# Attention with rotary embedding and a gated feed-forward layer: the scores of the first two blocks issued product by product, head against head, ahead of the other queries' transposes

## The chip, the cores and the metric

The kernel runs on one core of one Trainium2 chip. The metric is the device time of one execution in microseconds (us). The three executions of the kernel before took 718.72, 719.28 and 720.00 us; the median is 719.28 us. The profile is of one further execution of 719.76 us.

## The reference, cut to what matters

There are 4 batches, 8 heads, 576 positions and a head width of 64. Queries and keys are rotated, the scores are a softmax over 576 keys, and the result, laid out as 2304 tokens of 512 numbers, goes through a gated layer of width 1536:

```python
q_rot, k_rot = rotate(q), rotate(k)
scores = (1 / sqrt(64)) * q_rot @ k_rot.T
attn = exp(scores - max(scores)); attn = attn / (sum(attn) + 1e-9)
x = (attn @ v)            # as 2304 x 512
out = (silu(x @ w_gate) * (x @ w_val)) @ w_out
```

## The kernel before, in words

The 32 (batch, head) combinations are worked in 16 pairs of heads. A pair has 9 blocks of 128 queries: blocks 0 to 7 are four groups of queries for each of the two heads in turn (block 0 is head 0, block 1 is head 1, both of the first 128 queries), and block 8 holds the last 64 queries of both heads. Head 0 of a pair stands on partitions 0 to 63 and head 1 on partitions 64 to 127 of the tile `N`, which holds a rounded high part (index 1) and the rest, the low part (index 0), of the rotated and transposed queries and keys.

For each block TensorE makes the scores (`scores`): three terms, high by high, high by low and low by high, each as two products of 288 keys, added up in one PSUM buffer of two banks. There are two such buffers (`sc_p`, two in turn). VectorE takes the row maximum from the buffer (`peak`), ScalarE reads it again for the exponential with a row sum (`exp`), and then the buffer is free. Four TensorE transposes (`trans`) turn the result for the product with the values (`pv`).

The first blocks, among them 0 to 5, are "direct": each product contracts the 64 partitions of its head alone, so its stationary operand is 64x128. Later blocks stack the terms on 128 partitions (`QK`, `QZ`, `BD`), which `qk_stack` fills by eight DMAs on SyncE's queue (L313 to L320).

`start` (L210) writes the work of the first pair up to block 2 by hand, for all engines. The relevant part of it: `warm` (L223) issues idle 128x128 products on the identity to keep TensorE at work; `hi` and `lo` (L302, ScalarE; L306, VectorE) copy a transposed piece from PSUM into `N` as high part and low part; the first 128 queries and all keys are ready first, and the other queries are transposed at L253 after the rotation of them is done on GpSimd. The lists `warm` and `direct` of `PLAN` (L27) give the counts. Both score buffers serve VectorE's rotation as scratch (`tp`, `td`) before block 0 takes one of them.

After `start` a loop over all 144 blocks issues the steps. The order on GpSimd is the written one throughout, on SyncE up to block 47 and on TensorE up to block 8; the order of the others' instructions (VectorE's and ScalarE's from the loop on, TensorE's from block 9) is set at build time by a planner, which runs the program on a timeline of its own and takes what is ready by priority. From the end of the attention on, the order is written out again.

## Time and profile before

| | |
|---|---|
| median of three executions | 719.28 us |
| the profiled execution, its own time | 719.76 us |
| span of the profile, first to last instruction | 717.9 us |
| TensorE busy | 697.0 us (97%) |
| VectorE busy | 540.6 us (75%) |
| ScalarE busy | 409.6 us (57%) |
| GpSimd busy | 476.8 us (66%) |
| mean granted TensorE clock | 0.994 |

Busy times are of the engine's own work; PE is TensorE's products, PEld its loads of the stationary operand, DVE VectorE, ACT ScalarE, POOL GpSimd, SPq the DMA issues of SyncE. A product's busy time overlaps its neighbours', so the pitch from one to the next is read from the chain of waits, which counts each stretch once.

### The profile page before, as it was taken

Reading aid. Unit: us, or ns where it says so; the run is one execution under the profiler, and the core shown is the slowest. Engines: PE = TensorE matmul, PEld = TensorE weight load, DVE = VectorE, ACT = ScalarE, POOL = GpSimd, SP = SyncE. Lnnn points to the kernel's source line nnn. Section 1 sums busy time; section 2 is a strip of 40 time slices with the busy share of each in tenths; the row PEclk is TensorE's granted clock in tenths of the full one; section 3 lists DMA queues with packets and bytes.
Section 4 is the critical chain, followed back from the end, with each engine's and each line's share of the span. In section 5 each row is a group of like instructions: output and inputs, shape, how many; then the busy total and the mean of one; then the engine's idle time right before and its main releaser. Section 6 shows DMA issues by size and latency. Waiting matters only on the chain.

```text
span 717.9 us, 12738 instructions
## 1 busy us (share of the span) xinstructions
PE 697.0 (97%) x4342; PEld 656.7 (91%) x4342; DVE 540.6 (75%) x884; ACT 409.6 (57%) x892; POOL 476.8 (66%) x473
## 2 busy tenths in 40 slices
PE   7999999999999999998899999999999999999997
PEld 6999999999999998988899999999999877888887
DVE  5889898898898887848988778778677893464451
ACT  5889988888888886357433534424243332432331
POOL 8899799999999966649966576655675767200000
PEclk9999999999999999999999999999999999999999
DMA  6798899779887896862355555645638865787671
GB/s 195 195 232 204 218 227 253 199 202 249 233 215 196 201 269 165 248 202 101 121 168 171 177 163 173 193 147 165 185 115 272 280 245 169 306 284 223 205 220 30
DMA packets 111330, 143.86 MB, mean 200 GB/s; under 512 B 17809, under 2 KB 86049, under 8 KB 111265
## 3 DMA queue, kind: packets, MB, share of 16 engines
q1 hardware_dynamic: 106576, 137.64, 67.5%
q10 hardware_dynamic: 4688, 5.39, 2.3%
q8 instruction: 35, 0.57, 0.3%
q14 instruction: 31, 0.25, 0.1%
HBM read 76.35 MB, written 42.54 MB: 166 GB/s over the span
## 4 chain that ended last, share of the span: by engine, by line
PE 64%; DMA 10%; POOL 10%; DVE 8%; ACT 5%; issue 2%; SPq 1%; ACTq 0%; DVEq 0%; POOLq 0%
PE ch L824 28%; PE ch L941 13%; PE sc L343 7%; PE pv L459 6%; PE tr L419 5%; DMA HF<-hf 3%; PE ch L892 2%; POOL t L200 1%; DMA raw<-in_moe_w_gate_dram 1%; DMA QK<-N 1%; POOL rot L202 1%; DMA ht<-sv 1%; POOL rot L201 1%; PE tr L283 1%; POOL Xab L628 1%
## 5 line engine op out<-in xcount | busy, mean ns | idle before, releaser
L358 DVE TENSOR_REDUCE nmt<-sc 128x1 f32<-128x576 f32 x144 | 108.1, 751 | 20.0 <-PE sc L343 18.4
L376 ACT ACTIVATE E<-sc,nmt 128x576 f32<-128x576 f32 x128 | 97.3, 760 | 1.6 <-DVE nmt L358 1.4
L808 POOL TENSOR_TENSOR u<-u,z 128x384 f32<-128x384 f32 x30 | 30.5, 1018 | 72.9 <-DVE sg L808 72.9
L419 PE MATMUL tr<-ident,E 128*128 128x128 f32 x512 | 77.1, 273 | 0.5 <-DVE ET1l L421 0.2
L419 PEld LDWEIGHTS tr<-ident,E 128*128 128x128 f32 x512 | 61.1, 141 | 3.4 <-PE tr L283 1.3
L827 ACT COPY c<-ch 128x384 f32<-128x384 f32 x30 | 14.4, 480 | 84.7 <-PE ch L824 50.2
L200 POOL TENSOR_TENSOR t<-X,tab 128x256 f32<-128x256 f32 (+2 forms) x94 | 54.2, 597 | 10.1 <-DMA X<-in_qk_dram 6.4
L343 PE MATMUL sc<-QK 128*128 128x288 f32 x240 | 58.6, 325 | 1.7 <-ACT E L376 0.4
L420 ACT CAST ET2h<-tr 128x512 fp32r<-128x512 f32 x80 | 47.1, 589 | 15.5 <-PE tr L419 15.4
L421 DVE TENSOR_TENSOR ET2l<-tr,ET2h 128x512 fp32r<-128x512 f32 x80 | 53.1, 682 | 2.2 <-ACT ET2h L420 2.0
L678 DVE TENSOR_TENSOR hl<-hg,hh 128x384 fp32r<-128x384 f32 x44 | 25.8, 587 | 37.6 <-ACT hh L678 37.6
L941 PE MATMUL ch<-Oh,hh 128*128 128x512 f32 (+1 forms) x144 | 54.0, 375 | 0.0
L941 PE MATMUL ch<-Oh,hl 128*128 128x512 f32 (+1 forms) x144 | 53.9, 374 | 0.0
L941 PE MATMUL ch<-Ol,hh 128*128 128x512 f32 (+1 forms) x144 | 53.8, 374 | 0.0
L343 PE MATMUL sc<-N,QZ 128*128 128x288 f32 x240 | 51.3, 295 | 0.0
L202 POOL TENSOR_TENSOR rot<-rot,t 128x512 f32<-128x512 f32 (+2 forms) x47 | 47.0, 1000 | 3.7
L421 DVE TENSOR_TENSOR ET1l<-tr,ET1h 128x512 fp32r<-128x512 f32 x64 | 43.0, 685 | 6.8 <-ACT ET1h L420 6.5
L201 POOL TENSOR_TENSOR rot<-X,tab 128x512 f32<-128x512 f32 (+2 forms) x47 | 47.0, 1001 | 0.0
L808 DVE TENSOR_TENSOR sg<-ch,u 128x384 f32<-128x384 f32 x60 | 33.4, 556 | 16.5 <-PE ch L824 13.3
L678 ACT CAST hh<-hg 128x384 fp32r<-128x384 f32 x44 | 22.6, 514 | 39.3 <-DVE hg L928 39.3
L420 ACT CAST ET1h<-tr 128x512 fp32r<-128x512 f32 x64 | 36.9, 597 | 13.0 <-PE tr L419 13.0
L459 PE MATMUL pv<-ET2h,VS 128*128 128x320 f32 x128 | 40.7, 328 | 1.0 <-ACT ET2h L420 0.9
(413 smaller groups left out, 2418.9 us busy)
## 6 DMA issues: line engine op xcount, KB each, us to landing
QK<-N SPq DMA_DIRECT2D x64, 288.0 KB, 4.4
hg<-ht SPq DMA_DIRECT2D x22, 768.0 KB, 6.8
HF<-hf SPq DMA_DIRECT2D x12, 896.0 KB, 5.1
X<-in_qk_dram SPq DMA_DIRECT2D x15, 576.0 KB, 4.9
yd<-Y SPq DMA_DIRECT2D x31, 256.0 KB, 4.4
ht<-sg SPq DMA_DIRECT2D x20, 384.0 KB, 3.7
hf<-sg SPq DMA_DIRECT2D x20, 384.0 KB, 3.8
ht<-sg SPq DMA_DIRECT2D x20, 320.0 KB, 3.1
```

Of the source, the lines that this page charges most:

```text
L200: e.tensor_tensor(out=sel(t2, u), in0=sel(x, w), in1=tb(Sn, u), op=ALU.mult)
L201: e.tensor_tensor(out=o, in0=x, in1=tb(C, slice(0, D)), op=ALU.mult)
L343: nc.tensor.matmul(ps[:, g, 0:288], l, rr[:, o + g * 288:o + (g + 1) * 288], start=(x == 0), stop=(x == len(terms) - 1))
L358: nc.vector.tensor_reduce(out=nmcol, in_=ps[:, :, 0:288], axis=AX.XY, op=ALU.max, negate=True)
L376: nc.scalar.activation(out=E.rearrange("p (a b) -> p a b", a=2), in_=ps[:, :, 0:288], func=ACTF.Exp, bias=nmcol, scale=1.0, accum_out=self ...
L419: nc.tensor.transpose(ps[:, c], E[:, o + c * 128:o + (c + 1) * 128], self.ident)
L420: nc.scalar.copy(dst[0], src)
L421: nc.vector.tensor_tensor(out=dst[1], in0=src, in1=r32(dst[0]), op=ALU.subtract)
L459: nc.tensor.matmul(st["ps"][:, 0:w], VS[:, sl, :], t, start=(x == 0), stop=(x == last))
L808: add = lambda e, out, in0, in1: e.tensor_tensor(out=out, in0=in0, in1=in1, op=ALU.add)
L824: nc.tensor.matmul(acc, l[:, w, c * 128:(c + 1) * 128], r, start=(n == 0), stop=(n == 5))
L941: self.nc.tensor.matmul(ps, l[:, f], r[:, z], start=(n == 0), stop=(n == 3 * NFF - 1))
```

## The change

The scores of blocks 0 and 1 are no longer two calls of `scores` with the three transposes of the other queries (L253) between them. One new function takes both score buffers at once and issues the twelve products in turn: for each term and each half of the keys first head 0's, into the first buffer, then head 1's, into the second. The transposes follow behind all twelve. `hi`, `lo`, both `peak`, both `exp`, the idle products and everything on other engines keep their places in the written order. The argument of the first old call that could issue idle products behind its first term had a count of zero (`w[4]`).

```diff
         warm(w[3])
-        self.scores(0, False, lambda x: warm(w[4]) if x == 0 else None)
+        self.scores2()
         self.peak(0)
         ps = tr()
         for i in range(1, 4):
             T(ps[:, i * 128:(i + 1) * 128], rf[:, i * 128:(i + 1) * 128], self.ident)
-        self.scores(1, False)
         hi(ps[:, 128:512], 192, 384)
         lo(ps[:, 128:512], 192, 384)
         self.peak(1)
...
+    def scores2(self):
+        N = self.N[0]
+        ps = []
+        for n in range(2):
+            ps.append(self.sc_p.tile([128, 1024], FP32, name="sc").rearrange("p (a b) -> p a b", a=2))
+            self.sc[n] = ps[n]
+        for t, (x, y) in enumerate(((1, 1), (1, 0), (0, 1))):
+            for g in range(2):
+                for h in range(2):
+                    hs, ko = slice(64 * h, 64 * h + 64), (640, 576)[h]
+                    self.nc.tensor.matmul(ps[h][:, g, 0:288], N[hs, x, 64:192],
+                                          N[hs, y, ko + g * 288:ko + (g + 1) * 288], start=(t == 0), stop=(t == 2))
```

## Rows read from the trace of the kernel before

**Rows 1.** The page: busy time by engine, and the last chain's shares by engine.
```profile
PE 697.0 (97%) x4342; PEld 656.7 (91%) x4342; DVE 540.6 (75%) x884; ACT 409.6 (57%) x892; POOL 476.8 (66%) x473
...
PE 64%; DMA 10%; POOL 10%; DVE 8%; ACT 5%; issue 2%; SPq 1%; ACTq 0%; DVEq 0%; POOLq 0%
```
**Rows 2.** The chain of waits, 9 to 25 us: start, duration, what.
```profile
9.46 0.98 PE sc L343 x6
10.44 0.48 PE tr L253 x3
10.91 0.98 PE sc L343 x6
11.90 0.42 PE pv L223 x2
12.32 0.98 PE sc L343 x6
13.30 0.59 PE tr L419 x4
...
15.47 0.44 PE tr L283 x4
...
23.55 0.80 PE sc L343 x6
24.35 0.44 PE tr L419 x4
```
**Rows 3.** The timeline, all engines, 9.3 to 14 us: start, duration, what [idle before].
```profile
9.38 0.82 PEld L343 LDWEIGHTS sc<-N 64*128 64x128 f32 x6
...
10.47 0.76 DVE L358 TENSOR_REDUCE nmt<-sc 128x1 f32<-128x576 f32 x1 [0.69 <-PE sc L343]
...
10.95 0.48 ACT L302 CAST N<-tr 128x384 fp32r<-128x384 f32 x1 [1.02 <-PE tr L253]
...
11.33 0.75 ACT L376 ACTIVATE E<-sc,nmt 128x576 f32<-128x576 f32 x1
11.46 0.73 SPq L313 DMA_DIRECT2D QK<-N  x1
11.46 0.56 DVE L306 TENSOR_TENSOR N<-tr,N 128x384 fp32r<-128x384 f32 x1 [0.23 <-ACT N L302]
...
11.94 0.76 DVE L358 TENSOR_REDUCE nmt<-sc 128x1 f32<-128x576 f32 x1
11.96 0.20 ACT L376 ACTIVATION_READ_ACCUMULATOR E<-sc,nmt 128x1 f32 x1
...
12.25 0.82 PEld L343 LDWEIGHTS sc<-N 64*128 64x128 f32 x6
...
12.73 0.74 ACT L376 ACTIVATE E<-sc,nmt 128x576 f32<-128x576 f32 x1 [0.57 <-DVE nmt L358]
```
**Rows 4.** The timeline of VectorE, 8 to 10 us: the scratch's last reader.
```profile
8.34 0.29 DVE L202 TENSOR_TENSOR rot<-rot,sc 128x128 f32<-128x128 f32 x1
```
**Rows 5.** The timeline of SyncE's queue, 0 to 50 us, and of GpSimd.
```profile
22.02 0.60 SPq L313 DMA_DIRECT2D QK<-N  x1
...
30.21 0.59 SPq L169 DMA_DIRECT2D X<-in_qk_dram  x1
...
35.22 0.60 POOL L200 TENSOR_TENSOR t<-X,tab 128x64 f32<-128x64 f32 x2 [1.97 <-DMA X<-in_qk_dram]
```
**Rows 6.** The whole chain: block 8's scores of the sixth to eighth pair.
```profile
109.68 0.80 PE sc L343 x6
...
126.13 0.80 PE sc L343 x6
...
142.60 0.80 PE sc L343 x6
```
**Rows 7.** Stretches: busy time (instructions) of each engine, PEclk, DMA share, GB/s.
```profile
66.00:82.50 16.50, 15.48 (x122) 14.82 (x121) 15.87 (x29) 15.32 (x40) 12.60 (x14) 1.00 0.88 211
...
148.50:165.00 16.50, 16.49 (x132) 16.23 (x132) 14.50 (x24) 14.57 (x38) 15.78 (x21) 1.00 0.84 222
```
**Rows 8.** A stretch with a long TensorE wait, and that wait (us, times, longest).
```profile
274.00:278.00 4.00, 2.59 (x23) 2.35 (x21) 4.00 (x7) 3.87 (x10) 3.31 (x4) 1.00 0.41 129
...
PE ch L776 <- ACT Et L376: 1.4, 1, 1.4
```

## The prediction

> **What bounds the kernel now.** I read the page first: TensorE (PE) is busy 97% of the span, and the chain that ended last runs 64% on it [rows 1]. The reader should take from this only that a microsecond taken from TensorE may count, not that it does here: the change touches 3 us out of 718, and what it is worth is read from those. So the second view is the chain of waits around the change. From 9.46 to 13.9 us it is TensorE alone: scores of block 0, three transposes, scores of block 1, two idle products, scores of block 2, first transposes of the exponentials [rows 2]. Third is the timeline of all engines in the same stretch, since a chain shows one releaser and hides those that came a moment earlier [rows 3]. There the load for block 2's scores starts at 12.25 us, while ScalarE finishes the exponential of block 0, whose buffer block 2 needs, at 11.96 + 0.20 = 12.16 us. TensorE and ScalarE are 0.09 us apart at this point: two limits that are nearly equal, and the change relieves one of them. The second chain behind it is: transposes at L253, ScalarE's high copy (10.95), the exponential of block 0 (11.33), the free buffer (12.16). The maximum of block 0 (10.47 to 11.23) comes into the exponential just ahead of the copy's end.

> **The change part by part.** All sums go by the pitch of products, from the chain.

> *What it removes.* A block of six products with 64 contracted rows takes 0.98 us, a block of six of the same 288 columns with 128 rows takes 0.80 us (the blocks at 9.46 and 23.55) [rows 2]: 0.133 us a product, and 0.18 us more for turning to 64 rows. Four transposes behind a 64-row block take 0.59 us, in a row of transposes 0.44 us (at 13.30 and 15.47) [rows 2]: 0.15 us for turning back, and 0.11 us for a transpose, each with a load of its own. One trip out and back, 0.33 us, goes away, because blocks 0 and 1 are now one 64-row stretch.

> *What it adds: the length of the stretch of twelve products.* No row shows two products of different halves of the partitions next to each other, so the length has to be bounded. Lowest: each pair runs side by side, 6 x 0.133 + 0.18 = 0.98 us, as long as one block before. Highest of the plain cases: one after the other, 12 x 0.133 + 0.18 = 1.78 us. Between them: the products overlap but each needs its own load, and loads come no closer than the transposes show, 12 x 0.11 + 0.18 = 1.50 us. A fourth is a turn at each change of half: 11 changes at 0.15 to 0.18 us on top of 1.78, which is 3.4 to 3.8 us. I take 1.50 us, because the nearest row in which every product brings a new load is the transposes' 0.11 us.

> [...]

> *What is late then.* The three transposes stood behind six products and now stand behind twelve. They start later by the stretch less 0.98 us: 0 (side by side), 0.52 (loads), 0.80 (one by one), 2.4 to 2.8 (turns). Before, nothing else held them. With them move ScalarE's high copy, hence VectorE's low copy and second maximum (L306, 11.46; L358, 11.94), the exponential of block 0, which stands behind the copy in ScalarE's queue, the exponential of block 1 (12.73), and the first DMA of the stack on SyncE (L313, 11.46) [rows 3]. The buffer of block 0 comes free at 12.16 + shift, and 0.03 us later block 2's scores can start: 12.19 + shift against 12.25, so the net shift is -0.06, +0.46, +0.74 or +2.3 to +2.7 us. The other way into the exponential is milder: head 0's last product stands one place before the end, so the maximum ends at 11.23 + 0.52 - 0.11 = 11.64 us, before the copy frees ScalarE at 11.33 + 0.52 = 11.85.

> So what the change gains on TensorE, the second block's scores out of the way early and a 0.33 us trip saved, becomes a wait before block 2: in my case the three transposes (0.48 us) and the idle products end about 0.6 us before the buffer is free. The gain cannot be had, since no stretch of twelve can be shorter than block 0's six, and the chain transposes, copy, exponential starts behind it. That is why even full overlap is worth 0.06 us.

> *What costs nothing.* The stretch needs both buffers at once; their scratch use ends at 8.34 + 0.29 = 8.63 us [rows 4], before 9.38. The low parts of the keys and queries are needed only from the fifth and ninth product, later in the queue than before. No DMA and no GpSimd instruction is moved past another. The added wait of TensorE is short against one that this trace holds without harm: in 274 to 278 us it was busy 2.59 of 4.00 us, with one wait of 1.4 us, and the granted clock stayed at 1.00 [rows 8].

> *Does the shift reach the end?* Behind 13 us everything hangs on TensorE, ScalarE and VectorE of this chain; SyncE's second stack (22.02) and with it the load of the fourth pair's queries (30.21), on which GpSimd waits 1.97 us at 35.22 [rows 5], move with it. Later TensorE is full: 16.49 of 16.50 us in 148.5 to 165 [rows 7], so nothing there swallows or gives back. I let the 0.46 us through whole.

> Sum: the profiled execution's own 719.76 + 0.46 = 720.2 us. That execution lies 0.48 us over the median of the runs shown, so against the median: 719.28 + 0.46 = **719.7 us**. About 0.2%, 1.44 us, is what a measurement of this kernel tells from no change, so this is no change.

> **The rivals.**

> [...] *One by one (the change does not do what its order suggests):* +0.74, 720.0 us. For it: the pitch of 0.133 us has so far held for 64 and 128 rows alike. [...]

> *A turn at each change of half, slower.* If TensorE empties itself between the halves as it does between 64 and 128 rows, the twelve products take 3.4 to 3.8 us, block 2 starts 2.3 to 2.7 us late, and the time is 721.6 to 722.0 us. For it: the turns of 0.15 and 0.18 us exist. Against: they are seen only where the number of rows changes. It decides from about 0.06 us a change on: 0.74 + 11 x 0.064 = 1.44 us.

> *The plan falls another way.* VectorE's and ScalarE's order from the loop on and TensorE's from block 9 are made by a planner, whose view of the start is changed too. From 109.68 on, block 8's scores come every 16.45 us (126.13, 142.60) [rows 6]; from 23.55 to 109.68 [rows 2, 6] five pairs took 86.13 us, 3.9 us more than five such periods. In that part TensorE has holes (15.48 of 16.50 us in 66 to 82.5, where VectorE is busy 15.87 [rows 7]). That is 0.8 us a pair. A luckier order there could return the loss of two to five pairs, 1.6 to 3.9 us off the 719.7: 715.8 to 718.1 us. An unluckier one could lose as much again for two to four pairs, 1.6 to 3.1 us: 721.3 to 722.8 us. For both: ties of a tenth of a microsecond decide such orders. Against both: TensorE returned to the same period after every disturbance before.

> **How the numbers follow.** No change, by loads 0.28, side by side 0.21, one by one 0.15: together 0.64. Turns 0.08 and an unlucky plan 0.13 make slower 0.21. A lucky plan makes faster 0.15. The likeliest case alone has 719.2 to 720.0 us. To leave out no more than 2 in 10 the range reaches into both other sides: 717.4 (most of the lucky plans' nearer half) to 722.0 us (the turns, and the nearer half of the unlucky plans).

> **What would show it.** In the profile after, the twelve products as one stretch from 9.4 us: its length in the chain (0.98, 1.50, 1.78 or over 3 us) names the case. Right: TensorE shows a new wait before block 2's scores, released by the exponential of block 0 on ScalarE, and the exponential follows the high copy without a gap. Wrong: block 2's scores start before 12.1 us, or the transposes start before 10.37 us; then the chain over the copy was not the limit. The period of block 8's scores up to the sixth pair shows the plan: if 109.68 has moved by much more than the start of block 2 did, the plan changed and not the stretch. The forecast falls if the time leaves 717.8 to 720.7 us.

## The result, and the profile after

The changed kernel takes 723.61 us (median of 4 executions, 722.97 to 724.62), the kernel before beside it 719.64 us (718.72 to 720.04): ratio 1.0063, with a 95% interval of [1.0040, 1.0087] (intervals below are of the same kind). It is slower by about 4 us. My forecast was 719.7 us and no change, with a range that ended at 722.0. Three executions timed for the experiments below took 765 to 1148 us, at a mean granted clock of 0.56 to 0.85, and are left out of every count.

The page shows nearly the same busy sums as [rows 1]. The sums can't show the loss; what moved is the chain's share on TensorE, from 64% to 76%. Busy time and chain shares by engine:

```profile
PE 698.7 (97%) x4342; PEld 657.4 (91%) x4342; DVE 540.5 (75%) x884; ACT 409.3 (57%) x892; POOL 476.7 (66%) x473
...
PE 76%; DMA 7%; DVE 7%; ACT 6%; POOL 2%; issue 1%; SPq 1%; ACTq 0%; DVEq 0%; POOLq 0%
```

The chain of waits from 9 to 29 us (start, duration, what), to be laid beside [rows 2]. Line numbers have moved: L331 is the new paired stretch, L355 the other scores, L431 the transposes of the exponentials, L388 the exponential.

```profile
9.37 1.17 PE sc L331 x12
10.54 0.49 PE tr L253 x3
11.04 0.02 issue
11.06 0.48 ACT N L301
11.54 0.74 ACT E L388 x2
12.28 0.04 issue
12.32 0.79 PE sc L355 x4
13.11 0.26 PE tr L431
13.37 0.46 PE sc L355 x2
13.83 0.48 PE tr L431 x3
14.30 1.33 PE sc L355 x6
15.63 1.04 PE tr L431 x4
16.68 0.85 PE tr L282 x4
17.53 1.74 PE sc L355 x6
...
28.04 0.80 PE sc L355 x6
...
113.78 0.80 PE sc L355 x6
130.24 0.80 PE sc L355 x6
146.71 0.80 PE sc L355 x6
```

There are four things to see. The twelve products take 1.17 us. Block 2's scores start at 12.32 us, 0.07 after before (12.25 [rows 3]), but out of a wait. Those scores are now cut 4 and 2, with one transpose between, since the planner of TensorE's order let one of block 0's four transposes in. And from 14.3 us on everything is longer: six scores 1.33 and then 1.74 us where they took 0.98 [rows 2], four transposes 1.04 where they took 0.59. Block 8 starts at 28.04, 4.49 us later than before (23.55), and most of that distance is kept at 113.78, 130.24 and 146.71: 4.10, 4.11 and 4.11 us behind [rows 6]. What gives back the other 0.4 us was not traced.

The timeline of the same place (start, duration, what [idle before]) shows the wait, as foretold released by the exponential on ScalarE, which follows the copy without a gap:

```profile
9.30 1.24 PE L331 MATMUL sc<-N 64*128 64x288 f32 x12
...
11.06 0.48 ACT L301 CAST N<-tr 128x384 fp32r<-128x384 f32 x1 [1.21 <-PE tr L253]
...
11.43 0.75 ACT L388 ACTIVATE E<-sc,nmt 128x576 f32<-128x576 f32 x1
...
12.07 0.20 ACT L388 ACTIVATION_READ_ACCUMULATOR E<-sc,nmt 128x1 f32 x1
...
12.32 0.79 PE L355 MATMUL sc<-N 64*128 64x288 f32 x4 [1.08 <-ACT E L388]
```

The stretches say why everything after it is longer (columns as in [rows 7]: length; busy time and instructions of PE, PEld, DVE, ACT, POOL; granted clock; DMA share; GB/s):

```profile
9.30:12.30 3.00, 1.94 (x18) 1.44 (x17) 2.08 (x5) 1.76 (x4) 2.92 (x4) 1.00 0.62 197
12.30:14.76 2.46, 2.44 (x14) 1.83 (x15) 1.25 (x2) 1.25 (x3) 2.30 (x5) 1.00 0.75 142
14.76:18.20 3.44, 3.44 (x16) 2.83 (x15) 2.14 (x3) 2.39 (x7) 3.24 (x5) 0.50 1.00 219
18.20:21.60 3.40, 3.40 (x15) 2.79 (x14) 2.09 (x4) 1.56 (x4) 3.36 (x5) 0.50 0.58 119
21.60:25.00 3.40, 3.40 (x16) 3.11 (x16) 1.91 (x5) 1.73 (x6) 3.24 (x5) 0.50 0.39 104
25.00:28.00 3.00, 3.00 (x27) 3.00 (x26) 2.75 (x6) 2.66 (x8) 2.84 (x4) 1.00 0.05 12
```

For 10.24 us, from 14.76 to 25.00, TensorE's granted clock is 0.50, with 1.00 in the stretches ahead of it and behind it. TensorE has no idle moment in it, so nothing swallows the loss. The kernel before, in two of the same stretches, has TensorE full where it now waits (3.00 of 3.00 us against 1.94), and the clock at 1.00 throughout, with 25 instructions where 16 now fit:

```profile
9.30:12.30 3.00, 3.00 (x20) 2.31 (x18) 2.08 (x5) 1.85 (x5) 2.92 (x4) 1.00 0.59 197
14.76:18.20 3.44, 3.44 (x25) 2.89 (x25) 3.17 (x6) 2.99 (x9) 3.28 (x5) 1.00 1.03 226
```

The size fits. At the low clock six scores take 1.74 instead of 0.98 us and four transposes 1.04 instead of 0.59, both 1.77 times as long; 10.24 us at that pace hold 5.79 us of work, a loss of 4.45. The later start of block 2 adds 0.07, the split 0.33 (from block 2's first to block 3's first product it is 1.91 us here and 1.58 where the split is taken away, both by the timeline). That makes 4.85. Before, TensorE was idle for 0.30 of the 10 us from 16 to 26, which a slower TensorE fills: 4.55, measured 4.49.

### The profile page after: what moved, and what is told of

It reads as the page before. It is cut to its first block, busy times and chain, and to the rows that moved or that the text cites. A ratio compares the mean times of both kernels' runs of the same rounds, so it can differ in the third digit from the quotient of the medians.

```text
span 721.3 us, 12739 instructions
## 1 busy us (share of the span) xinstructions
PE 698.7 (97%) x4342; PEld 657.4 (91%) x4342; DVE 540.5 (75%) x884; ACT 409.3 (57%) x892; POOL 476.7 (66%) x473
## 4 chain that ended last, share of the span: by engine, by line
PE 76%; DMA 7%; DVE 7%; ACT 6%; POOL 2%; issue 1%; SPq 1%; ACTq 0%; DVEq 0%; POOLq 0%
PE ch L836 28%; PE ch L953 13%; PE pv L471 11%; PE sc L355 11%; PE tr L431 8%; DMA HF<-hf 3%; PE tr L282 2%; ACT E L388 1%; DMA ht<-sv 1%; ACT N L301 1%; DVE HF L894 1%; PE ch L788 1%; POOL fl L690 1%; DMA hg<-ht 1%; DVE T2l L690 1%
## 5 line engine op out<-in xcount | busy, mean ns | idle before, releaser
L370 DVE TENSOR_REDUCE nmt<-sc 128x1 f32<-128x576 f32 x144 | 108.3, 752 | 21.4 <-PE sc L355 18.9
L388 ACT ACTIVATE E<-sc,nmt 128x576 f32<-128x576 f32 x128 | 97.6, 763 | 1.1 <-DVE nmt L370 1.0
L431 PE MATMUL tr<-ident,E 128*128 128x128 f32 x512 | 78.8, 278 | 0.4 <-DVE ET1l L433 0.2
L431 PEld LDWEIGHTS tr<-ident,E 128*128 128x128 f32 x512 | 62.3, 143 | 3.8 <-issue 1.5
L200 POOL TENSOR_TENSOR t<-X,tab 128x256 f32<-128x256 f32 (+2 forms) x94 | 54.0, 596 | 14.3 <-DMA X<-in_qk_dram 10.7
L355 PE MATMUL sc<-QK 128*128 128x288 f32 x240 | 59.1, 328 | 1.3 <-ACT E L388 0.4
L355 PE MATMUL sc<-N,QZ 128*128 128x288 f32 x240 | 51.7, 297 | 0.0
```

The costliest lines, as they stand in the source:

```text
L200: e.tensor_tensor(out=sel(t2, u), in0=sel(x, w), in1=tb(Sn, u), op=ALU.mult)
L355: nc.tensor.matmul(ps[:, g, 0:288], l, rr[:, o + g * 288:o + (g + 1) * 288], start=(x == 0), stop=(x == len(terms) - 1))
L370: nc.vector.tensor_reduce(out=nmcol, in_=ps[:, :, 0:288], axis=AX.XY, op=ALU.max, negate=True)
L388: nc.scalar.activation(out=E.rearrange("p (a b) -> p a b", a=2), in_=ps[:, :, 0:288], func=ACTF.Exp, bias=nmcol, scale=1.0, accum_out=self ...
L431: nc.tensor.transpose(ps[:, c], E[:, o + c * 128:o + (c + 1) * 128], self.ident)
```

## The experiments

The theory is **C**: the new wait of 1.08 us brings TensorE's clock down (in its first form the wait alone; the two extra turns of the split came in later). Against it stood **O**, that the order itself (both blocks' scores ahead of the transposes) costs it, and **P**, that two products side by side bring the clock down, as denser work. Later came **S** and **T** on what the split does, and **H**, **L** and **L2** on why the low clock lasts so long.

Whether an execution had the fall is read from its mean granted clock, as 10.24 us at half lower the mean by 10.24 x 0.5 / 721 = 0.007. All 88 executions of the kernel before that were timed beside these runs had 0.994 to 1.000. I call 0.993 and less a fall. The line is drawn just under that kernel's lowest, so its own count of none follows from it; but its two traces show no low clock from 10 to 328 us either.

**Filling the wait.** The changed kernel with five idle products (128 rows) ahead of block 2's scores in place of one; then with three; then with none, further below. (The trace lists each idle product as two.)

```diff
-    warm=[9, 0, 1, 2, 0, 1],
+    warm=[9, 0, 1, 2, 0, 5],
```

> The changed kernel with five idle products on the identity instead of one between the three transposes and block 2's scores; the wait there (1.08 us in the changed kernel) should shrink to about 0.2 us. Theory C (the wait before block 2 makes the granted clock fall to half from 14.8 to 25 us, and that is the loss): no fall before 30 us, block 8 of the first pair back from 27.88 to about 23.5 us, time 719.2 to 720.3 us. Rival O (the loss comes from the new order itself, the split transposes and the moved copy): unchanged, 723 to 724.5 us. [...]

Measured: wait 0.18 us, 718.06 us, ratio 0.9981 [0.9967, 0.9995]; a fall in 1 of 11 executions. The whole loss is gone with pairing and order as they were, so O and P fall. The one execution that was profiled was the one that fell, from 15.7 to 25.9 us; its wait, by the timeline of TensorE:

```profile
12.54 0.79 PE L355 MATMUL sc<-N 64*128 64x288 f32 x4 [0.18 <-ACT E L388]
```

> The same with three idle products; about 0.65 us of the wait is left. Theory C: the clock holds if the size of the wait decides, 719.2 to 720.3 us; if the fall needs less wait than that, some of the 4 us comes back in part of the runs only. Rivals O and P: 723 to 724.5 us.

Measured, with three idle products: wait 0.63 us, 719.04 us, 1.0000 [0.998, 1.002]; falls in 3 of 12. A middle wait gives a middle count.

**The order without the pairing.** The kernel before, with both blocks' scores ahead of the transposes, one block behind the other.

```diff
-        self.scores(0, False, lambda x: warm(w[4]) if x == 0 else None)
+        self.scores(0, False)
+        self.scores(1, False)
         self.peak(0)
...
-        self.scores(1, False)
```

> The kernel before with the scores of blocks 0 and 1 one after the other ahead of the transposes, each as its own call: the change's order without its pairing. Twelve products take about 1.78 us, the transposes start 0.8 us later, block 2 about 0.7 us later, after a wait of about 1 us. Theory C: the wait is there, the clock falls as in the changed kernel, 723.5 to 725 us. Rival P: no pairing, no fall, 719.6 + 0.7 = 720.3 us. Rival O: 723 to 724.5 us with the clock at full speed.

Measured: the twelve products 1.82 us, wait 1.08 us, 723.35 us, 1.0048 [1.0024, 1.0072]; falls in 9 of 12. Without pairing the fall is there all the same. That the stretch takes what the prediction reckoned for products one by one, 1.78 us, is luck. By the starts in the trace the third product waits for the low copy of the keys (10.52 us, 0.32 behind the second, where 0.13 is the pitch), and block 1's first two products, at 10.73 and 10.96 us, start among block 0's last four, so part of the two blocks ran side by side here too. Against P the runs with the wait filled and the wait alone therefore count for more.

**The wait alone.** The kernel before, its TensorE order untouched, with two ScalarE copies that nobody needs ahead of block 0's exponential.

```diff
+        nc.scalar.copy(self.VS[0][:, :, 0:64], self.VR)
+        nc.scalar.copy(self.VS[0][:, 0:5, 0:64], self.VR[:, 0:5])
         self.exp(0)
```

> The kernel before with two more copies on ScalarE (640 and 320 columns, about 1.1 us together) ahead of the exponential of block 0; TensorE's order is that of the kernel before, and only a wait of about 1 us before block 2's scores is new. Theory C: the clock falls, 719.6 + 1.1 + about 4 = 724 to 725.5 us. Rivals O and P: no fall, 720.2 to 721 us.

Measured: wait 1.01 us, 724.98 us, 1.0080 [1.0064, 1.0097]; falls in 6 of 6, in the trace from 13.7 to 27.4 us. This is the plainest proof for C: nothing of the change is in this kernel but a wait; TensorE's 4342 instructions come in the same order as before. TensorE in that trace (timeline), where six scores take 1.79 us straight behind the wait:

```profile
13.69 1.79 PE L345 MATMUL sc<-N 64*128 64x288 f32 x6 [1.01 <-ACT E L378]
15.41 1.11 PE L421 MATMUL tr<-ident,E 128*128 128x128 f32 x4
16.45 1.81 PE L345 MATMUL sc<-N 64*128 64x288 f32 x6
```

**The changed kernel and the kernel before once more.**

> The changed kernel once more, for how often the clock falls at the start. Theory C, in the form that the first four kernels left (a wait of 1.0 us before block 2 makes the fall frequent, 0.2 us makes it rare; an execution with the fall takes 721.4 us or more, one without it 720 us or less): most executions, 9 of 12 or more, at 721.4 us or over; median 722.5 to 724 us. If the fall were a matter of the chip or the day: a spread like that of the kernel before, around 719 us.

Measured: 723.03 us, 1.0063 [1.0043, 1.0083], wait 1.08 us, falls in 5 of 5; with the first four executions 9 of 9. The kernel before, once more:

> The kernel before, profiled once more, to see what differs between two executions of one program. Granted clock at full speed from its first rise to beyond 300 us, block 8 of the first pair at 23.3 to 24.3 us; the short falls near 331 and 358 us and the wait for the data read from the scratch in memory near 315 us may differ by 1 to 2 us.

Measured: 717.65 us in one execution, mean clock 0.997, block 8 at 23.58 us; no low clock between 10 and 300 us, and one short fall near 329.

**The split taken away.** Block 0's four transposes are kept where the program writes them, so that block 2's scores stay whole.

```diff
-            nc.tensor.transpose(ps[:, c], E[:, o + c * 128:o + (c + 1) * 128], self.ident)
+            T = nc.tensor.transpose(ps[:, c], E[:, o + c * 128:o + (c + 1) * 128], self.ident)
+            if n == 0:
+                self.tc.keep_in_program_order(T)
```

> The changed kernel with the first block's four transposes held behind block 2's scores, as in the kernel before; the planner had put one of them between its products, which costs two turns more. The wait of 1.08 us before block 2 stays. Theory C: the fall stays frequent, most executions over 721.4 us, median 722 to 724 us. Rival O in its last form (the split transposes are what tips the clock): falls become rare, 718 to 719.5 us.

Measured: wait 1.08 us as before, 719.19 us, 1.0020 [1.0003, 1.0038]; falls in only 3 of 12. C in its first form, the wait alone, missed here; the time is what O in its last form had foretold. The timeline shows the wait and then full speed:

```profile
12.86 1.06 PE L355 MATMUL sc<-N 64*128 64x288 f32 x6 [1.08 <-ACT E L388]
13.85 0.66 PE L431 MATMUL tr<-ident,E 128*128 128x128 f32 x4
14.44 1.06 PE L355 MATMUL sc<-N 64*128 64x288 f32 x6
```

So the split matters too. Either it is needed (T), or its two turns count like the wait, as time in which TensorE does nothing (S: wait plus 0.33 us for each trip out and back, over the one trip that all these kernels have between block 0 and block 2).

> The same with the wait filled by five idle products as well: pairing, no wait, no split. Theory C: falls are rare, 1 of 12 or none; 0.35 us less than with the fill alone, 717.3 to 718.5 us median, and so 0.1 to 0.3% under the kernel before. If the fill alone was faster than the kernel before by luck only: 718.8 to 719.8 us.

> Pairing with the wait filled and without the split once more, against the kernel before: no fall in any execution, 717 to 719 us median, ratio 0.998 to 1.000.

Measured, without split and with five idle products: wait 0.19 us; 717.34 us, 0.9989 [0.9975, 1.0002], then 718.56 us, 0.9992 [0.9974, 1.0009]; falls in 0 of 23. It can't be told from the kernel before, nor from the version with the split, at 0.9981.

> The changed kernel with the transposes held behind block 2's scores (no split) and with no idle product at all before block 2: the wait grows from 1.08 to about 1.3 us. Account S (wait and turns add up to TensorE's empty time after 9.4 us, and the more there is, the oftener the clock falls: 0.5 us 1 of 11, 1.0 us 3 of 12, 1.4 us 9 of 9): the falls become more than 3 of 12, some 6 to 9, median 721 to 723.5 us. Account T (the split itself tips it, the wait alone does not): 3 of 12 or fewer, median 718.5 to 719.5 us.

Measured, without split and without any idle product: wait 1.30 us, 722.19 us, 1.0030 [1.0008, 1.0052]; falls in 8 of 12. TensorE, by the timeline:

```profile
13.13 1.05 PE L355 MATMUL sc<-N 64*128 64x288 f32 x6 [1.30 <-ACT E L388]
```

No split is needed, so T falls. By S the kernels line up:

```
kernel                          wait + trips     sum    falls
after, no split, five idle      0.19             0.19   0 of 23
before                          0.00 + 0.33      0.33   0 of 88
after, five idle                0.18 + 0.33      0.51   1 of 11
after, three idle               0.63 + 0.33      0.96   3 of 12
after, no split                 1.08             1.08   3 of 12
after, no split, no idle        1.30             1.30   8 of 12
wait alone                      1.01 + 0.33      1.34   6 of 6
not paired                      1.08 + 0.33      1.41   9 of 12
after                           1.08 + 0.33      1.41   9 of 9
```

S is fitted to these counts, apart from the run with the wait of 1.30 us, which it foretold. It says how likely a fall is here; it doesn't say which execution falls. The kernels with fewer idle products also have less full-height work ahead of block 2. Whether idle products of 64 rows would fill the wait as well was not tried, so empty time and missing full-height work are told apart only by the run with the wait alone, which keeps all of its products.

**How long the low clock lasts.** In the six traces with a fall so far its start differs (13.7 to 15.9 us), and its length is 10.2 us in five and 13.7 in the one with the earliest start, the wait alone. What they share is the end: the clock is back 1.0 to 2.6 us after the first scores with 128 contracted rows (block 6; up to there TensorE has 64-row scores and transposes). The first try put two idle products behind each of blocks 3, 4 and 5 of the changed kernel.

> The changed kernel with two idle 128x128 products behind the scores of blocks 3, 4 and 5 each, that is within the stretch in which its clock is at half. If the clock answers to how full the array is and not to TensorE's busy time in the profile (which is already 100% in that stretch): the stretch at half clock ends after 3.4 or 6.8 us and not after 10.2 us, and the time is 720 to 722.5 us in spite of 1.3 to 2.6 us more work. If not: still 10.2 us or more, 724.5 to 726 us.

Measured: 722.2 us, 1.0058 [1.0036, 1.0080], falls in 4 of 8, but not in the profiled execution. The time lies in the first of the two ranges, but a fall cut to 3.4 or 6.8 us would lower the mean clock by 0.002 to 0.005 only, so the count can't tell fewer falls from shorter ones, and the run settles nothing. The second try used the kernel with the wait alone, which fell every time, and put six idle products behind block 3's scores, once with 128 rows and once with 64:

```diff
+        def idle(rows):
+            for _ in range(6):
+                nc.tensor.matmul(pw[:, 0:128], self.ident[0:rows], self.ident[0:rows], start=True, stop=True)
...
             at.scores(n + 1)
+            if n + 1 == 3:
+                at.idle(128)
```

> The kernel before with the two ScalarE copies ahead of the first exponential (the 1 us wait of the run with the wait alone, which fell in 6 of 6 executions, at half clock from 13.7 to 27.4 us), and six idle products of 128 rows and 128 columns behind the scores of block 3, that is inside the fall, at about 18.2 us. Theory H (the clock stays at half as long as TensorE gets only 64-row products and transposes, and returns soon after the first full-height products: in six traces with a fall it came back 1.0 to 2.6 us after the first 128-row scores, whatever the start): the clock is back at 19 to 21.5 us, the half-clock stretch is 5.5 to 8 us, and the time is 1 to 3 us below that of the kernel with six 64-row idle products at the same place. Rival L (a fall runs for some 10 to 14 us whatever is issued): half clock up to 24 us or later, and both idle kernels take the same time within 1 us.

> The same with 64 rows in the six idle products in place of 128, same columns and same place. Theory H: they don't help; half clock until 1 to 2.6 us after the first 128-row scores, so to about 29 us, a half-clock stretch of 13 to 16 us, time 726 to 728 us. Rival L: half clock to about 24 to 27.5 us, the same as with 128 rows.

> The kernel with the 1 us wait and six idle products of 64 rows once more, for a trace with a fall (the profiled execution before was the one of five without). Theory H: half clock from about 14.5 us until 1 to 3 us after the first 128-row scores, so beyond 24 us, a stretch of 10 to 15 us. Rival L2 (idle products of any height end a fall some 4 us after they begin): back before 22 us.

> The kernel with the 1 us wait and six idle products of 128 rows once more. Theory H: the clock is back by 22 us again, before the first 128-row scores, a stretch of 5.5 to 8 us; a stretch of over 9 us would say that the first trace was chance.

> As the run before last, with 64 rows: Theory H beyond 24 us where the execution falls, Rival L2 before 22 us.

Measured: with 128 rows 724.72 us, 1.0091 [1.0070, 1.0111], falls in 5 of 5 in its two runs (by the mean clock, a weaker sign where a fall is shorter); with 64 rows 724.96 us, 1.0089 [1.0067, 1.0112], falls in 6 of 7 in its three. Up to the fall both are the kernel with the wait alone, which so falls in 17 of 18. The first 64-row trace had no fall. In the others the low clock ran from 14.6 to 21.4 and from 14.9 to 21.8 us with 128 rows, and from 15.0 to 28.6 and from 15.3 to 29.0 us with 64 rows: 6.8 us against 13.6. (Of the twelve entries of the six 64-row products the planner put three between block 3's scores, the others behind them.) The mean clocks of all falling executions agree (0.9906 against 0.9862, that is 6.4 us at half on average between them). The stretches of one trace each, 64 rows first:

```profile
15.00:21.50 6.50, 6.50 (x32) 5.61 (x31) 2.66 (x4) 3.12 (x7) 6.26 (x8) 0.50 0.84 180
22.00:24.50 2.50, 2.50 (x11) 1.89 (x10) 1.18 (x2) 0.61 (x2) 2.34 (x6) 0.50 0.51 141
24.50:28.00 3.50, 3.50 (x15) 3.22 (x15) 2.00 (x4) 1.82 (x6) 3.34 (x4) 0.50 0.00 0
```
```profile
22.00:24.50 2.50, 2.50 (x18) 2.17 (x18) 2.19 (x4) 1.51 (x4) 2.42 (x4) 1.00 0.43 129
24.50:28.00 3.50, 3.19 (x26) 2.77 (x26) 3.33 (x7) 3.19 (x9) 3.34 (x5) 1.00 0.00 0
```

And the products behind which the clock came back in the second of them, and the first 128-row scores, which came only afterwards (timeline of TensorE):

```profile
17.39 2.93 PE L226 MATMUL pv<-ident 128*128 128x128 f32 x12
...
25.30 0.50 PE L349 MATMUL sc<-QK 128*128 128x288 f32 x2
```

H holds; L (a fixed length) and L2 (idle products of any height) fall. The expected times were off: at the first product of the feed-forward part the 128-row kernels are 1.7 to 2.7 us ahead (283.50 and 284.37 us against 286.04 and 286.19), as H had it, but at the end of the falling executions only 0.4 us (medians 724.71 and 725.09). One of the 128-row traces has one more short low stretch, from 363.1 to 366.5 us, and from 315 to 330 us TensorE idles for 0.84 and 0.69 us in the 128-row traces and not at all in the 64-row ones; I have not accounted for the rest.

## Why the prediction was wrong

*The limit, and what is late next: right.* The chain over transposes, high copy and exponential held, and the gain on TensorE became a wait before block 2, 1.08 us where I had some 0.6. My own rows give 0.82, not 0.6: a buffer free at 12.68 less 9.46 + 1.50 + 0.48 + 0.42. Those 0.42 us of the idle products hold a turn that is no longer there: behind the transposes they take 0.21.

*The length of the stretch: the other case, at no cost.* Twelve products took 1.17 us, against 0.98 side by side and 1.50 by loads, the case that I took. In the trace the two products of a pair start 0.002 to 0.004 us apart (9.301 and 9.304, 9.537 and 9.540, 9.745 and 9.748 us), so the halves do run together. The last three pairs start 0.13 us apart; the rest, some 0.2 us, lies around the third pair, which starts 0.21 us behind the second and 0.24 ahead of the fourth. It needs the low copy of the keys, which VectorE makes from 9.00 to 9.69 us. The net shift was +0.07 in place of my +0.46 us. A turn at each change of half did not come: the two loads of a pair start 0.003 to 0.004 us apart, as the products do. Where the number of rows changes, the loads pause for 0.16 to 0.17 us with nothing in the profile to wait for (timeline, PEld at 10.37, 10.84, 11.83 and 13.23 us in the kernel before, at 10.47 and 13.04 in the changed one).

*The planner: one local effect on TensorE, no other.* It split block 2's scores, worth 0.33 us and, by the run without the split, much of the fall. I had written that TensorE's order up to block 8 is the written one; the trace shows that it isn't where `start` meets the loop. The shift of 4.10 to 4.11 us at blocks 8 of the sixth to eighth pair is constant, and behind the split TensorE's instructions come in the same order as before to the end: neither the lucky nor the unlucky plan of my rivals came.

*The step that failed* is in "What costs nothing": "The added wait of TensorE is short against one that this trace holds without harm", by the 1.4 us wait of [rows 8], through which the clock stayed at 1.00. I took one stretch as a bound for another. What stands around the two waits differs. Behind the wait of [rows 8] there are products of 128 rows (timeline of TensorE in the kernel before), behind the wait at 12 us 64-row scores and transposes, and in the runs with idle products inside the fall those of 128 rows cut the low clock to 6.8 us, while those of 64 rows left it at 13.6. That the same difference is why no fall came at 274 us is likely but was not tried. Where before has a fall in the feed-forward part, among 128-row products, it is short: 3.4 us at 331 and again at 358 us (6.8 us in two of the other traces, near 333 and 336 us).

```profile
277.89 0.44 PE L776 MATMUL ch<-xa0h,w0h 128*128 128x384 f32 x1 [1.41 <-ACT Et L376]
```

So the forecast lacked a term: the low clock, 4.45 us by the rows above, with a probability that goes from 0 of 88 to 9 of 9 as 1.08 us of TensorE's time is left empty and two turns come in; with the wait of 1.08 us and no split it is 3 of 12.

*Open:* which executions fall when the empty time is middling (3 of 12), and why 64-row scores did not bring the clock back here although TensorE shows as busy for 3.40 of 3.40 us. On the first the record holds a hint. By the clock records of the traces the granted clock first reaches full speed at another moment in each execution, from 5.96 to 9.11 us (6.44 in the profile before, 7.94 in the one after), and in the ten traces with an early fall the fall began the later, the later that was. Of the three traces with a wait of 1.0 to 1.1 us and no early fall, two have the earliest such moments (5.96 and 6.20 us), but the third, without the split, the latest (9.11). No run here sets that moment.

## What to carry to other kernels

Work taken off TensorE in a place where another engine was the limit gave a wait here, and the wait cost more than the work was worth: the time saved on TensorE came back as a wait of 1.08 us, and with it a loss of 4. Look at what TensorE does behind the new wait: where it is half-height products and transposes, try to fill the wait with full-height idle products (five of them brought the falls from 9 of 9 to 1 of 11, and without the split from 3 of 12 to 0 of 23), and time it some ten times, since some executions of one kernel fall and others don't (3 of 12). A wait elsewhere in the trace that did no harm is no bound by itself: in the kernel before the clock stayed at 1.00 through 1.4 us ahead of 277.9 us, and in the changed one it fell in 9 of 9 executions behind 1.08 us ahead of 12.3 us.
